# A retention layer and two MLPs on one core: six units of attention in plain float32, and no arithmetic on GpSimd

## The chip, the cores and the metric

The kernel runs on one core of one Trainium2 chip. A core has a matrix engine (TensorE, PE in the rows), a vector engine (VectorE, DVE), a scalar engine (ScalarE, ACT), GpSimd (POOL) and SyncE (SP), which here only issues transfers. Each engine takes its own instructions strictly in the order in which the program lists them, and waits on semaphores for the others. The metric is the device time of one execution in microseconds; lower is better. Before the change three runs gave 1268.5 to 1269.55 us, median 1269.53 us.

## The reference

```python
def _attn_ref(q, k, v):                     # B, H, S, D = 4, 8, 768, 64
    gamma = 1.0 - 2.0 ** (-5.0 - np.arange(H))
    for t in range(S):
        state = gamma * state + outer(k[t], v[t])       # one 64x64 state for each batch entry and head
        y[t] = (1 / sqrt(D)) * q[t] @ state
...
x = attn.transpose(0, 2, 1, 3).reshape(3072, 512)
h = x @ w_in;  x = np.maximum(0.01 * h, h) @ w_out      # first MLP, 512 -> 2048 -> 512
h = np.maximum(x @ w_in2, 0);  return (h * h) @ w_out2  # second MLP
```

The MLP weights arrive as float64, and the kernel makes float32 of them on the chip.

## The kernel before, in words

**Attention.** The recurrence is done in chunks of 256 tokens. A *unit* is one chunk of one batch entry; there are 12 (units 0 to 3 are the first chunks of the four entries, 4 to 7 the second, 8 to 11 the third), each with four pairs of heads. For each pair a row of 128x1024 floats (q, k, v, and k the other way round) is loaded, `prep_pair` multiplies the decays into q and v, and then for each head: `scores` (k against q, two key blocks of 128 against 256 queries), `soften` (causal mask, on DVE), `values` (masked scores against v, plus the older state against q), and, after a pair's second head, `outer` (adds the chunk to the state) and `combine` (writes y into the MLP's input).

**Two ways of multiplying.** The first three units (`WHOLE = 3`) give PE plain float32 operands. The profile shows two records on PE for each such product. All other products take each operand as a sum of two `float32r` parts, high and low, and multiply three pairs of parts (or stack the parts along the contraction or the output, in the attention). The parts are made by a copy on ACT and a subtraction on DVE or GpSimd: `kh`/`kl`, `q2`, `v2`, the masked scores `ph_pl`, the state `w2`, the weights `wih`/`wil` and `woh`/`wol`, the activations `gh`/`gl`.

**MLPs.** Tokens go in six blocks of 512; each MLP passes over six blocks, each in 16 *steps* j of 128 hidden columns (the first block has 21 steps: its first five run once on 256 tokens and again on the others). A step has 12 products into `h` (L402), an activation (L416 to L427) and 12 into `acc` (L462). In all 197 steps. Units 0 to 3 are used by the first two blocks; after the first eight heads one head goes with each step, until step 77: unit 4 with steps 14 to 21, unit 5 with 22 to 29, units 6 to 11 with 30 to 77 (`place`).

**Weights.** `convert` makes float32 of a half tile (128x512) of float64: two ACT operations (L314, L315), three DVE operations (L316, L317, L320) and an integer addition (L324), which is GpSimd's for the first MLP and for half of the second's half tiles, otherwise DVE's. The 32 half tiles of the first MLP are converted in the first steps, the second's from step 81 on, in block 5. `split_w` makes the two parts of a weight tile for every step anew; the subtraction (L365) is GpSimd's in the first block of each MLP, else DVE's. `soften`'s subtraction (L203) is GpSimd's in unit 3.

**Order.** The loops are written step by step; a scheduler then orders the instructions of each engine, so the rows of an engine are not in the order of the code. SP's queue takes the weight loads (`sg`) and the pairs' rows (`r`, `re`, `kn`) in one line.

Of the kernel before, what the change touches and what calls it, by code (L numbers as in the profile page):

```python
# [14 lines left out]
ALU = mybir.AluOpType  # L15
# [10 lines left out]
T = 512                      # tokens in a block of the MLPs  # L26
# [4 lines left out]
WHOLE = 3                    # units whose products are taken in float32 as it is: PE has the time for it then  # L31
HS = 5                       # steps of the first block on its first unit alone, in float32 as it is too
LEAD = 6                     # steps by which the heads run ahead of the block that takes them
AHEAD = 2                    # steps by which the first MLP's weights run ahead
AHEAD2 = 4                   # and the second's
PARTS = 4                    # units from which on GpSimd leaves the scores' parts to DVE
FLOOR = 2.0 ** -15 * 1.125   # its float32 pattern is the high word of float64's 2^-126

# columns of one pair's row in `attn`: q^T | k^T twice | v | k
Q0, K0, V0, N0, AW = 0, 256, 768, 1024, 1280  # L40
FW = 1024                    # the same, with k^T once, of a row in `first`
# [3 lines left out]
def retention_then_two_mlps(  # L45
# [27 lines left out]
    ph_pl = [const.tile([P, 2, 512], F32R, name=f"ph_pl{h}") for h in range(2)]  # L73
    state = const.tile([P, B, NP, D], F32, name="state")

# [18 lines left out]
    def load_pair(up):  # L94
        u, p = up
        k = ups.index(up)
        if u < WHOLE:
            if k % 4:
                t = slot(k % 4, [P, FW], F32, "re")
            else:  # L100
                t = a_p.tile([P, FW], F32, tag="r", name="r", bufs=1)
            if k == 0:
                nc.sync.dma_start(out=t[:, 0:2 * C], in_=first[k, :, 0:2 * C])
                nc.sync.dma_start(out=t[:, 2 * C:FW], in_=first[k, :, 2 * C:FW])
            else:
                nc.sync.dma_start(out=t, in_=first[k])
            raw[up] = (t[:, 0:C], t[:, C:2 * C], t[:, 2 * C:3 * C], t[:, 3 * C:FW])
            return
        row = attn[k - WHOLE * NP]
        t = a_p.tile([P, N0], F32, tag="r", name="r", bufs=1)  # L110
        nc.sync.dma_start(out=t, in_=row[:, 0:N0])
        kn = None
        if chunk(u) < NC - 1:
            kn = a_p.tile([P, 2 * P], F32, tag="kn", name="kn")
            nc.sync.dma_start(out=kn, in_=row[:, N0:AW])
        raw[up] = (t[:, Q0:K0], t[:, K0:V0], t[:, V0:N0], kn)

    def prep_pair(up):
        """Decays go to the queries and values; all but the first units' operands in two parts."""
# [11 lines left out]
        if u < WHOLE:  # L131
            prep[up] = (qs, k, vs)
            return
        kr = k.rearrange("p (h s) -> p h s", h=2)
        kh = [a_p.tile([P, C], F32R, tag="kh", name="kh") for h in range(2)]
        kl = [a_p.tile([P, C], F32R, tag="kl", name="kl") for h in range(2)]
        q2 = [a_p.tile([P, C], F32R, tag="q2", name="q2", bufs=3) for h in range(2)]
        v2 = [a_p.tile([P, 2, 2, D], F32R, tag="v2", name="v2", bufs=3) for h in range(2)]
        for h in range(2):
            nc.scalar.copy(kh[h], kr[:, h])  # L140
        for h in range(2):
            nc.vector.tensor_tensor(out=kl[h], in0=kr[:, h], in1=kh[h].bitcast(F32), op=ALU.subtract)  # L142
# [8 lines left out]
        for h in range(2):  # L151
            nc.scalar.copy(v2[h][:, :, 0], vs[:, :, h])
        for h in range(2):
            nc.vector.tensor_tensor(
                out=v2[h][:, :, 1], in0=vs[:, :, h], in1=v2[h][:, :, 0].bitcast(F32), op=ALU.subtract
            )
# [15 lines left out]
    def scores(hu):  # L172
        u, p, h = hu
        if u < WHOLE:
            qs, k, vs = prep[u, p]
            a = slice(64 * h, 64 * h + 64)
            sc = ps_h.tile([P, 512], F32, tag="h", name="sc")
            nc.tensor.matmul(out=sc[:, 128:256], lhsT=k[a, P:2 * P], rhs=qs[a, P:2 * P], start=True, stop=True)
            nc.tensor.matmul(out=sc[:, 256:512], lhsT=k[a, 0:P], rhs=qs[a], start=True, stop=True)
        else:  # L180
            q2, kh, kl, v2, vs, w2 = prep[u, p]
            sc = ps_h.tile([P, 512], F32, tag="h", name="sc")
            for sb in (1, 0):
                o = C * (1 - sb)
                for n, kk in enumerate((kh, kl)):
                    nc.tensor.matmul(  # L186
                        out=sc[:, o:o + C], lhsT=kk[h][:, sb * P:(sb + 1) * P], rhs=q2[h],
                        start=n == 0, stop=n == 1,
                    )
        sc_ps[hu] = sc  # L190

    def soften(hu):
        """Scores under the causal mask."""
        sc = sc_ps.pop(hu)
        pm = a_p.tile([P, 384], F32, tag="pm", name="pm")
        nc.vector.tensor_tensor(out=pm, in0=sc[:, 128:512], in1=mk, op=ALU.mult)  # L196
        if hu[0] < WHOLE:
            p_sb[hu] = pm
            return
        t = ph_pl[hu[2]]  # L200
        nc.scalar.copy(t[:, 0, 128:512], pm)
        eng = nc.gpsimd if hu[0] < PARTS else nc.vector
        eng.tensor_tensor(  # L203
            out=t[:, 1, 128:512], in0=pm, in1=t[:, 0, 128:512].bitcast(F32), op=ALU.subtract
        )

    def values(hu):
# [3 lines left out]
        if u < WHOLE:  # L211
# [3 lines left out]
            nc.tensor.matmul(out=y, lhsT=vs[:, 0, h], rhs=pm[:, 128:384], start=True, stop=False)  # L215
# [5 lines left out]
        if w2 is not None:  # L221
            nc.tensor.matmul(out=y, lhsT=w2[:, h].rearrange("p a e -> p (a e)"), rhs=q2[h], start=True, stop=False)
            start = False
        for n in range(2):
            for sb in range(2):
                o = C * (1 - sb)
                nc.tensor.matmul(  # L227
                    out=y, lhsT=v2[h][:, sb].rearrange("p a e -> p (a e)"), rhs=ph_pl[h][:, n, o:o + C],
# [4 lines left out]
    def outer(up):  # L233
        """Adds the chunk's keys and values to the state."""
# [61 lines left out]
    def convert():  # L296
        """The nearest float32 of a half tile of float64, out of its two words.

        The high word has the sign, the exponent and 20 bits of the fraction. Its
        pattern, as a float, keeps the order of the magnitudes and is held at or  # L300
        above that of 2^-126, the least that float32 holds. The low word, rounded
        to its upper three bits, is added to that as an integer.
        """
# [3 lines left out]
        if half == 0:  # L307
# [6 lines left out]
        nc.scalar.activation(out=r, in_=hi.bitcast(F32), func=AF.Abs)  # L314
        nc.scalar.activation(out=lo, in_=lo, func=AF.Copy, scale=2.0 ** -29)  # L315
        nc.vector.tensor_scalar(out=r, in0=r, scalar1=FLOOR, scalar2=None, op0=ALU.max)  # L316
        nc.vector.tensor_scalar(  # L317
            out=ru, in0=ru, scalar1=3, scalar2=0x3FFFFFF8, op0=ALU.logical_shift_left, op1=ALU.bitwise_and,
        )
        nc.vector.scalar_tensor_tensor(  # L320
            out=ru, in0=hi, scalar=0xC0000000, in1=ru, op0=ALU.bitwise_and, op1=ALU.bitwise_or,
        )
        eng = nc.vector if lay == 1 and (m % 4 < 2) else nc.gpsimd
        eng.tensor_tensor(out=ru, in0=ru, in1=lo, op=ALU.add)  # L324
# [10 lines left out]
    # a step: (layer block, j, first and last column)  # L335
# [10 lines left out]
    widens = {HS}                # the step where old and new columns meet  # L346
# [7 lines left out]
    def split_w(i, half):  # L354
# [9 lines left out]
        eng = nc.gpsimd if n in (0, NB) else nc.vector  # L364
        eng.tensor_tensor(out=lo, in0=src, in1=hi.bitcast(F32), op=ALU.subtract)  # L365
# [64 lines left out]
    def emit_out(i):  # L430
# [14 lines left out]
        # a bank's first product clears it for all its columns, also those of later steps  # L445
# [69 lines left out]
    conv2 = first_step[NB - 1]   # from here on the first MLP's weights go, tile by tile  # L515
# [5 lines left out]
    def after(hu):  # L521
        """What follows a head's values."""
# [16 lines left out]
    for t in ph_pl:  # L539
        nc.gpsimd.memset(t[:, :, 0:128].bitcast(F32), 0.0)  # L540
# [20 lines left out]
    for i in range(N):  # L561
# [27 lines left out]
        elif i >= conv2 - AHEAD2:  # L589
            j = i - conv2  # L590
            converted_to(2 * NJ + min(int((j + AHEAD2) / 0.85), 2 * max(j, 0) + 2))
# [5 lines left out]
def _tables():  # L597
    """Decays of the heads and the causal mask: of shapes alone."""
# [54 lines left out]
```

## Time and profile before

| | |
|---|---|
| median of three runs | 1269.53 us (1268.5 to 1269.55) |
| span of the profiled execution, first to last instruction | 1267.9 us; 0.6 to 1.7 us of a run's time lie around such a span |
| busy: PE, weight loads, DVE, ACT, POOL | 95%, 78%, 72%, 56%, 14% of the span |
| POOL instructions | 126, all before 220 us or between 620 and 860 us |
| PE matmul records | 5660 |

Matmuls are pipelined, so the mean duration of a record is longer than its pace; the distance between the starts of neighbours, or the time of a run of many, shows the pace. DVE instructions, too, are recorded some 0.08 us longer than the distance at which they follow each other. A block of the MLPs is 16 steps, so the distance between the last products of two blocks shows what a block took.

### The profile page before, as it was taken

Reading aid. Unit: us, or ns where it says so; the run is one execution under the profiler, and the core shown is the slowest. Engines: PE = TensorE matmul, PEld = TensorE weight load, DVE = VectorE, ACT = ScalarE, POOL = GpSimd, SP = SyncE. Lnnn points to the kernel's source line nnn. Section 1 sums busy time; section 2 is a strip of 40 time slices with the busy share of each in tenths; the row PEclk is TensorE's granted clock in tenths of the full one; section 3 lists DMA queues with packets and bytes.
Section 4 is the critical chain, followed back from the end, with each engine's and each line's share of the span. In section 5 each row is a group of like instructions: output and inputs, shape, how many; then the busy total and the mean of one; then the engine's idle time right before and its main releaser. Section 6 shows DMA issues by size and latency. Waiting matters only on the chain.

```text
span 1267.9 us, 15585 instructions
## 1 busy us (share of the span) xinstructions
PE 1210.7 (95%) x5660; PEld 995.2 (78%) x5660; DVE 915.9 (72%) x1669; ACT 711.3 (56%) x1482; POOL 171.7 (14%) x126
## 2 busy tenths in 40 slices
PE   6887797999999999999999989999999999999998
PEld 4566586888888888888887768888888888888886
DVE  5999988988988988898599972454555644555543
ACT  4555655766766776776467754444444544444443
POOL 1266662000000000000012264400000000000000
PEclk9898898999999999999999999999999999999999
DMA  8534211121111111111034410000000000000000
GB/s 296 200 136 161 98 59 42 42 63 42 42 59 34 34 50 34 41 44 50 1 99 151 150 50 1 1 34 1 1 34 1 34 1 1 34 1 1 34 1 33
DMA packets 23404, 69.36 MB, mean 55 GB/s; under 512 B 2848, under 2 KB 5664, under 8 KB 23328
## 3 DMA queue, kind: packets, MB, share of 16 engines
q1 hardware_dynamic: 23328, 68.37, 15.6%
q8 instruction: 44, 0.72, 0.2%
q14 instruction: 32, 0.26, 0.1%
HBM read 62.07 MB, written 6.29 MB: 54 GB/s over the span
## 4 chain that ended last, share of the span: by engine, by line
PE 78%; DVE 15%; issue 4%; DMA 2%; ACT 1%; SPq 0%; POOL 0%; DVEq 0%; ACTq 0%; POOLq 0%
PE acc L462 36%; PE h L402 35%; DVE w L320 3%; PE y L227 2%; PE sc L186 2%; DVE w L317 2%; DVE w L316 2%; DVE gl L427 1%; DVE pm L196 1%; DVE g L417 1%; DMA r<-attn 1%; DVE kl L142 1%; DVE q L148 1%; DVE qs L124 1%; DVE vs L125 1%
## 5 line engine op out<-in xcount | busy, mean ns | idle before, releaser
L402 PE MATMUL h<-xh,wih 128*128 128x512 f32 (+1 forms) x768 | 303.2, 395 | 11.8 <-DVE pm L196 9.3
L402 PE MATMUL h<-xh,wil 128*128 128x512 f32 (+1 forms) x768 | 302.7, 394 | 4.3 <-POOL wil L365 2.4
L402 PE MATMUL h<-xl,wih 128*128 128x512 f32 (+1 forms) x768 | 301.0, 392 | 0.1
L363 ACT CAST woh<-w 128x512 fp32r<-128x512 f32 x192 | 119.3, 622 | 161.2 <-PE acc L462 159.5
L365 DVE TENSOR_TENSOR wol<-w,woh 128x512 fp32r<-128x512 f32 x160 | 111.0, 694 | 118.4 <-ACT woh L363 117.2
L402 PEld LDWEIGHTS h<-xh,wih 128*128 128x128 f32 x768 | 147.0, 191 | 43.3 <-DVE pm L196 10.2
L402 PEld LDWEIGHTS h<-xh,wil 128*128 128x128 f32 x768 | 147.2, 192 | 36.8 <-DVE wil L365 4.7
L402 PEld LDWEIGHTS h<-xl,wih 128*128 128x128 f32 x768 | 146.7, 191 | 30.5 <-DVE xl L381 1.1
L427 DVE TENSOR_TENSOR gl<-g,gh 128x512 fp32r<-128x512 f32 (+1 forms) x192 | 144.9, 755 | 28.8 <-ACT gh L426 14.0
L426 ACT CAST gh<-g 128x512 fp32r<-128x512 f32 (+1 forms) x192 | 118.1, 615 | 59.6 <-DVE g L420 29.6
L324 POOL TENSOR_TENSOR w<-w,sg 128x512 uint32<-128x512 uint32 x48 | 70.2, 1464 | 575.3 <-DVE w L320 532.1
L420 DVE SCALAR_TENSOR_TENSOR g<-h,g 128x512 f32<-128x512 f32 x96 | 66.2, 690 | 89.0 <-ACT g L419 88.3
L363 ACT CAST wih<-w 128x512 fp32r<-128x512 f32 x192 | 117.8, 614 | 11.9 <-PE h L402 8.6
L365 DVE TENSOR_TENSOR wil<-w,wih 128x512 fp32r<-128x512 f32 x160 | 109.7, 686 | 5.8 <-ACT wih L363 5.5
L462 PE MATMUL acc<-gl,woh 128*128 128x512 f32 (+1 forms) x388 | 107.3, 386 | 4.2 <-DVE gl L427 4.2
L462 PE MATMUL acc<-gh,woh 128*128 128x512 f32 (+1 forms) x388 | 107.3, 390 | 1.6 <-ACT gh L426 1.5
L462 PE MATMUL acc<-woh,gh 128*128 128x512 f32 x384 | 105.7, 389 | 1.1 <-DVE ys L472 1.1
L419 ACT ACTIVATE g<-h 128x512 f32<-128x512 f32 x96 | 57.4, 598 | 87.7 <-PE h L402 80.2
L462 PE MATMUL acc<-gh,wol 128*128 128x512 f32 (+1 forms) x388 | 106.1, 383 | 0.0
L462 PE MATMUL acc<-wol,gh 128*128 128x512 f32 x384 | 105.6, 389 | 0.0
L462 PE MATMUL acc<-woh,gl 128*128 128x512 f32 x384 | 105.6, 389 | 0.0
L416 ACT ACTIVATE g<-h 128x512 f32<-128x512 f32 (+1 forms) x101 | 58.0, 575 | 70.2 <-PE h L402 42.6
(89 smaller groups left out, 1806.5 us busy)
## 6 DMA issues: line engine op xcount, KB each, us to landing
sg<-w SPq DMA_DIRECT2D x64, 512.0 KB, 3.6
r<-attn SPq DMA_DIRECT2D x36, 512.0 KB, 3.5
out<-os SPq DMA_DIRECT2D x24, 256.0 KB, 2.0
re<-first SPq DMA_DIRECT2D x9, 512.0 KB, 4.9
kn<-attn SPq DMA_DIRECT2D x20, 128.0 KB, 2.1
r<-first SPq DMA_DIRECT2D x2, 512.0 KB, 6.3
r<-first SPq DMA_DIRECT2D x2, 256.0 KB, 2.8
qt<-qtab SPq DMA_DIRECT2D x1, 384.0 KB, 6.4
```

What stands on the lines that cost most here:

```text
L186: nc.tensor.matmul(out=sc[:, o:o + C], lhsT=kk[h][:, sb * P:(sb + 1) * P], rhs=q2[h], start=n == 0, stop=n == 1,)
L320: nc.vector.scalar_tensor_tensor(out=ru, in0=hi, scalar=0xC0000000, in1=ru, op0=ALU.bitwise_and, op1=ALU.bitwise_or,)
L324: eng.tensor_tensor(out=ru, in0=ru, in1=lo, op=ALU.add)
L363: nc.scalar.copy(hi, src)
L365: eng.tensor_tensor(out=lo, in0=src, in1=hi.bitcast(F32), op=ALU.subtract)
L402: nc.tensor.matmul(out=hp[:, :c1 - c0], lhsT=a[:, kb * P:(kb + 1) * P], rhs=b[:, c0:c1], start=kb == 0 and k == 0, stop=kb == KB - 1 and k ...
L416: nc.scalar.activation(out=g[:, :m], in_=hp[:, :m], func=AF.Copy, scale=LEAK)
L419: nc.scalar.activation(out=g[:, :m], in_=hp[:, :m], func=AF.Relu)
L420: nc.vector.scalar_tensor_tensor(out=g[:, :m], in0=hp[:, :m], scalar=0.0, in1=g[:, :m], op0=ALU.max, op1=ALU.mult)
L426: nc.scalar.copy(gh[:, :m], g[:, :m])
L427: nc.vector.tensor_tensor(out=gl[:, :m], in0=g[:, :m], in1=gh[:, :m].bitcast(F32), op=ALU.subtract)
L462: nc.tensor.matmul(out=o, lhsT=lhsT, rhs=rhs, start=start and k == 0, stop=stop and k == 2)
```

## The change

- `WHOLE` is 6: units 3, 4 and 5 also take plain float32 products, without parts. Units 4 and 5 have an older state; it is copied by ACT onto the two diagonal blocks of a 128x128 tile (`s_diag`, two of them, cleared once by GpSimd), and one product of 256 columns for both heads of a pair adds its part to y.
- The rows of units 4 and 5 are loaded in turn into `r` and one of the free block slots (before: `r` alone).
- `convert` has three DVE operations: ACT now scales the high word by a power of two in place of taking its magnitude, the maximum (L316) is gone, the shift has no mask, and the integer addition is always DVE's.
- `split_w`'s and `soften`'s subtractions are always DVE's. GpSimd only clears the two tiles.
- In the units still split, the second key block is multiplied with the 128 queries that can see it (before: 256, of which 128 were masked to zero), in scores and values. `kh`/`kl` and `v2` are made for two heads in one operation each.
- The second MLP's half tiles are converted at one a step (before: 1.18 a step), with a due time.

```diff
-WHOLE = 3
+WHOLE = 6
-    ph_pl = [const.tile([P, 2, 512], F32R, name=f"ph_pl{h}") for h in range(2)]
+    s_diag = [const.tile([P, P], F32, name=f"s_diag{n}") for n in range(2)]
@@ load_pair
-            if k % 4:
-                t = slot(k % 4, [P, FW], F32, "re")
+            if k % 4 and (k < 4 * NP or k % 2):
+                t = slot(k % 4 if k < 2 * NP else 2 + k % 2 if k < 4 * NP else 3, [P, FW], F32, "re")
@@ prep_pair
         if u < WHOLE:
+            if chunk(u):
+                for h in range(2):
+                    a = slice(64 * h, 64 * h + 64)
+                    nc.scalar.copy(s_diag[p % 2][a, a], state[a, u % B, p])
@@ scores
             for sb in (1, 0):
-                o = C * (1 - sb)
+                o, c = (P, P) if sb else (C, 0)
                 for n, kk in enumerate((kh, kl)):
                     nc.tensor.matmul(
-                        out=sc[:, o:o + C], lhsT=kk[h][:, sb * P:(sb + 1) * P], rhs=q2[h],
+                        out=sc[:, o:o + C - c], lhsT=kk[:, h * C + sb * P:h * C + (sb + 1) * P], rhs=q2[h][:, c:C],
@@ values
+            if past and h == 0:
+                nc.tensor.matmul(out=y_ps[u, p][:, 0], lhsT=s_diag[p % 2], rhs=qs, start=True, stop=False)
...
-                    out=y, lhsT=v2[h][:, sb].rearrange("p a e -> p (a e)"), rhs=ph_pl[h][:, n, o:o + C],
+                    out=y[:, c:C], lhsT=v2[:, sb, h].rearrange("p a e -> p (a e)"), rhs=t[:, n, o:o + C - c],
@@ convert
-        nc.scalar.activation(out=r, in_=hi.bitcast(F32), func=AF.Abs)
+        nc.scalar.activation(out=r, in_=hi.bitcast(F32), func=AF.Copy, scale=2.0 ** -112)
-        nc.vector.tensor_scalar(out=r, in0=r, scalar1=FLOOR, scalar2=None, op0=ALU.max)
-        nc.vector.tensor_scalar(
-            out=ru, in0=ru, scalar1=3, scalar2=0x3FFFFFF8, op0=ALU.logical_shift_left, op1=ALU.bitwise_and,
-        )
+        nc.vector.tensor_scalar(out=ru, in0=ru, scalar1=3, scalar2=None, op0=ALU.logical_shift_left)
-        eng = nc.vector if lay == 1 and (m % 4 < 2) else nc.gpsimd
-        eng.tensor_tensor(out=ru, in0=ru, in1=lo, op=ALU.add)
+        nc.vector.tensor_tensor(out=ru, in0=ru, in1=lo, op=ALU.add)
@@ split_w
-        eng = nc.gpsimd if n in (0, NB) else nc.vector
-        eng.tensor_tensor(out=lo, in0=src, in1=hi.bitcast(F32), op=ALU.subtract)
+        nc.vector.tensor_tensor(out=lo, in0=src, in1=hi.bitcast(F32), op=ALU.subtract)
@@ the order of it all
-            converted_to(2 * NJ + min(int((j + AHEAD2) / 0.85), 2 * max(j, 0) + 2))
+            due = 2 * (i + 1 + AHEAD - first_step[NB]) + 1
+            converted_to(2 * NJ + max(min(j + AHEAD2, 2 * max(j, 0) + 2), due))
```

How this stands in the engines' orders, at two places. The first is DVE in the first steps, where half tiles of weights are converted (`w`) between the heads of the first units (`pm` is a head's masked scores, `qs`/`vs` a pair's decayed operands, `xl` a part of the MLP's input). Before:

```order
L316 TENSOR_SCALAR w<-w 128x512
L317 TENSOR_SCALAR w<-w 128x512
L316 TENSOR_SCALAR w<-w 128x512
L125 TENSOR_TENSOR vs<-re,vt 128x256
L317 TENSOR_SCALAR w<-w 128x512
L320 SCALAR_TENSOR_TENSOR w<-sg,w 128x512
L196 TENSOR_TENSOR pm<-sc,mk 128x384
L317 TENSOR_SCALAR w<-w 128x512
L196 TENSOR_TENSOR pm<-sc,mk 128x384
L124 TENSOR_TENSOR qs<-re,qt 128x256
L320 SCALAR_TENSOR_TENSOR w<-sg,w 128x512
```

And now, in the same steps:

```order
L314 TENSOR_SCALAR w<-w 128x512
L315 SCALAR_TENSOR_TENSOR w<-sg,w 128x512
L124 TENSOR_TENSOR vs<-re,vt 128x256
L192 TENSOR_TENSOR pm<-sc,mk 128x384
L374 TENSOR_TENSOR xl_551<-xs_137,xh_550 128x512
L315 SCALAR_TENSOR_TENSOR w<-sg,w 128x512
L318 ISA w<-sg,w 128x1024
L192 TENSOR_TENSOR pm<-sc,mk 128x384
L123 TENSOR_TENSOR qs<-re,qt 128x256
L318 ISA w<-sg,w 128x1024
L314 TENSOR_SCALAR w<-w 128x512
```

One of the two scalar operations of a half tile is gone from DVE, and GpSimd's integer addition stands there now (the `ISA` rows, 128x1024 half words).

The second place is PE in a step of units 6 and later, around one split head (`sc` scores, `y` values, `w` the older state, `sp` the outer product). Before:

```order
L186 MATMUL sc<-q_3681,kh 128x256
L186 MATMUL sc<-q_3681,kl 128x256
L243 MATMUL sp<-vs,kn 128x128 x2
L462 MATMUL acc<-gh,woh 128x512 x4
L462 MATMUL acc<-gh,wol 128x512 x2
L222 MATMUL y<-q_3680,w_3696 128x256
L227 MATMUL y<-ph_pl_89,v_3682 128x256 x4
L222 MATMUL y<-q_3681,w_3696 128x256
```

And now:

```order
L182 MATMUL sc<-q_2470,kh 128x128
L182 MATMUL sc<-q_2470,kl 128x128
L182 MATMUL sc<-q_2470,kh 128x256
L182 MATMUL sc<-q_2470,kl 128x256
L224 MATMUL y<-ph,v_2320 128x256
L224 MATMUL y<-ph,v_2320 128x128
L455 MATMUL acc<-gh,woh 128x512 x4
L455 MATMUL acc<-gh,wol 128x512 x4
L455 MATMUL acc<-gl,woh 128x512 x4
```

Of the eight products of a head's scores and values four now have 128 columns; there are 192 such products in the 48 heads of units 6 to 11.

## Rows read from the trace of the kernel before

**Rows 1.** Stages: length; busy (count) of PE, PEld, DVE, ACT, POOL; clock, DMA, GB/s

```profile
0.00:20.00 20.00, 12.14 (x54) 7.72 (x55) 6.06 (x16) 7.45 (x18) 0.77 (x6) 1.00 0.86 318
20.00:160.00 140.00, 114.78 (x522) 84.99 (x522) 135.78 (x201) 81.28 (x172) 74.30 (x54) 0.88 0.44 156
160.00:220.00 60.00, 52.23 (x303) 44.73 (x302) 50.91 (x99) 34.88 (x90) 25.05 (x19) 0.94 0.17 53
...
240.00:640.00 400.00, 400.00 (x2009) 339.82 (x2008) 337.49 (x748) 267.15 (x639) 0.15 (x1) 1.00 0.13 41
640.00:750.00 110.00, 101.60 (x424) 79.41 (x422) 107.55 (x174) 74.33 (x132) 35.95 (x22) 0.98 0.38 129
```

**Rows 2.** Chain that ended last, in order of time: start, length, what

```profile
161.29 3.57 DMA r<-attn
...
649.03 5.44 PE acc L462 x24
...
750.28 4.84 PE acc L462 x20
...
837.41 5.44 PE acc L462 x24
```

**Rows 3.** Timeline, 64.9 to 66.6 us: start, length, engine, line

```profile
64.94 1.35 POOL L324 TENSOR_TENSOR w<-w,sg 128x512 uint32<-128x512 uint32 x1 [2.15 <-DVE w L320]
65.06 1.51 DVE L317 TENSOR_SCALAR w<-w 128x512 uint32<-128x512 uint32 x1
```

**Rows 4.** Timeline, 71.3 to 72.5 us, DVE

```profile
71.36 0.68 DVE L320 SCALAR_TENSOR_TENSOR w<-sg,w 128x512 uint32<-128x512 uint32 x1
71.96 0.41 DVE L316 TENSOR_SCALAR w<-w 128x512 f32<-128x512 f32 x1
...
72.30 0.54 DVE L196 TENSOR_TENSOR pm<-sc,mk 128x384 f32<-128x384 f32 x1
```

**Rows 5.** Groups by line on DVE, 0 to 220 us: busy us, mean ns

```profile
L317 DVE TENSOR_SCALAR w<-w 128x512 uint32<-128x512 uint32 x33 | 31.6, 957 | 0.4
...
L427 DVE TENSOR_TENSOR gl<-g,gh 128x512 fp32r<-128x512 f32 x11 | 14.8, 1343 | 0.3 <-ACT gh L426 0.3
```

**Rows 6.** Groups by line on DVE, 240 to 640 us

```profile
L365 DVE TENSOR_TENSOR wol<-w,woh 128x512 fp32r<-128x512 f32 x62 | 42.8, 690 | 7.6 <-ACT woh L363 6.4
L427 DVE TENSOR_TENSOR gl<-g,gh 128x512 fp32r<-128x512 f32 x61 | 41.7, 684 | 0.9 <-ACT gh L426 0.2
...
L142 DVE TENSOR_TENSOR kl<-r,kh 128x256 fp32r<-128x256 f32 x53 | 22.0, 415 | 0.0
...
L317 DVE TENSOR_SCALAR w<-w 128x512 uint32<-128x512 uint32 x2 | 0.9, 427 | 0.1
L324 DVE CUSTOM_DVE_ANT_0 w<-sg,w 128x1024 uint16<-128x1024 uint16 x1 | 0.7, 681 | 0.0
```

**Rows 7.** Groups by line on POOL, 0 to 220 us

```profile
L324 POOL TENSOR_TENSOR w<-w,sg 128x512 uint32<-128x512 uint32 x32 | 44.9, 1404 | 80.6 <-DVE w L320 46.8 <-DMA sg<-w 20.0 <-ACT gh L426 4.0
```

**Rows 8.** Timeline on PE, two stretches: one plain head, one split head's scores

```profile
75.41 0.65 PE L215 MATMUL y<-pm,vs 128*64 128x256 f32 x2
75.89 0.38 PE L216 MATMUL y<-pm,vs 128*64 128x128 f32 x2
76.20 0.48 PE L178 MATMUL sc<-qs,re 64*128 64x128 f32 x2
76.53 0.59 PE L179 MATMUL sc<-qs,re 64*128 64x256 f32 x2
...
105.41 0.28 PE L186 MATMUL sc<-q,kh 128*128 128x256 f32 x1
105.53 0.28 PE L186 MATMUL sc<-q,kl 128*128 128x256 f32 x1
```

**Rows 9.** Groups by line on PE, 0 to 220 us

```profile
L402 PE MATMUL h<-xh,wih 128*128 128x512 f32 (+1 forms) x71 | 30.6, 431 | 9.3 <-DVE pm L196 9.3
```

**Rows 10.** The page's part 4, by engine

```profile
PE 78%; DVE 15%; issue 4%; DMA 2%; ACT 1%; SPq 0%; POOL 0%; DVEq 0%; ACTq 0%; POOLq 0%
```

More of the change, by code (lines that the diff above doesn't have):

```diff
@@ L35 @@
 AHEAD2 = 4
-PARTS = 4
-FLOOR = 2.0 ** -15 * 1.125
 Q0, K0, V0, N0, AW = 0, 256, 768, 1024, 1280
@@ L131, in prep_pair @@
         if u < WHOLE:
+            if chunk(u):
+                for h in range(2):
+                    a = slice(64 * h, 64 * h + 64)
+                    nc.scalar.copy(s_diag[p % 2][a, a], state[a, u % B, p])
             prep[up] = (qs, k, vs)
             return
-        kr = k.rearrange("p (h s) -> p h s", h=2)
-        kh = [a_p.tile([P, C], F32R, tag="kh", name="kh") for h in range(2)]
-        kl = [a_p.tile([P, C], F32R, tag="kl", name="kl") for h in range(2)]
+        kh = a_p.tile([P, 2 * C], F32R, tag="kh", name="kh", bufs=1)
+        kl = a_p.tile([P, 2 * C], F32R, tag="kl", name="kl", bufs=1)
         q2 = [a_p.tile([P, C], F32R, tag="q2", name="q2", bufs=3) for h in range(2)]
[L138 to L142, printed above, removed]
+        v2 = a_p.tile([P, 2, 2, 2, D], F32R, tag="v2", name="v2", bufs=2)
+        nc.scalar.copy(kh, k)
+        nc.vector.tensor_tensor(out=kl, in0=k, in1=kh.bitcast(F32), op=ALU.subtract)
         for h in range(2):
@@ L150, in prep_pair @@
             )
[L151 to L155, printed above, removed]
-            )
+        nc.scalar.copy(v2[:, :, :, 0], vs)
+        nc.vector.tensor_tensor(out=v2[:, :, :, 1], in0=vs, in1=v2[:, :, :, 0].bitcast(F32), op=ALU.subtract)
         w2 = None
@@ L199, in soften @@
             return
[L200 to L205, printed above, removed]
+        t = p_sb[hu] = a_p.tile([P, 2, 384], F32R, tag="ph", name="ph")
+        nc.scalar.copy(t[:, 0], pm)
+        nc.vector.tensor_tensor(out=t[:, 1], in0=pm, in1=t[:, 0].bitcast(F32), op=ALU.subtract)
     def values(hu):
@@ L214, in values @@
             y = y_ps[u, p][64 * h:64 * h + 64, 0]
-            nc.tensor.matmul(out=y, lhsT=vs[:, 0, h], rhs=pm[:, 128:384], start=True, stop=False)
+            past = chunk(u) > 0
+            if past and h == 0:
+                nc.tensor.matmul(out=y_ps[u, p][:, 0], lhsT=s_diag[p % 2], rhs=qs, start=True, stop=False)
+            nc.tensor.matmul(out=y, lhsT=vs[:, 0, h], rhs=pm[:, 128:384], start=not past, stop=False)
             nc.tensor.matmul(out=y[:, P:2 * P], lhsT=vs[:, 1, h], rhs=pm[:, 0:128], start=False, stop=True)
@@ L223, in values @@
             start = False
+        t = p_sb.pop(hu)
         for n in range(2):
             for sb in range(2):
-                o = C * (1 - sb)
+                c, o = (P, 0) if sb else (0, P)
                 nc.tensor.matmul(
-                    out=y, lhsT=v2[h][:, sb].rearrange("p a e -> p (a e)"), rhs=ph_pl[h][:, n, o:o + C],
+                    out=y[:, c:C], lhsT=v2[:, sb, h].rearrange("p a e -> p (a e)"), rhs=t[:, n, o:o + C - c],
                     start=start, stop=n == 1 and sb == 1,
@@ L313, in convert @@
         ru = r.bitcast(U32)
-        nc.scalar.activation(out=r, in_=hi.bitcast(F32), func=AF.Abs)
+        nc.scalar.activation(out=r, in_=hi.bitcast(F32), func=AF.Copy, scale=2.0 ** -112)
         nc.scalar.activation(out=lo, in_=lo, func=AF.Copy, scale=2.0 ** -29)
-        nc.vector.tensor_scalar(out=r, in0=r, scalar1=FLOOR, scalar2=None, op0=ALU.max)
-        nc.vector.tensor_scalar(
-            out=ru, in0=ru, scalar1=3, scalar2=0x3FFFFFF8, op0=ALU.logical_shift_left, op1=ALU.bitwise_and,
-        )
-        nc.vector.scalar_tensor_tensor(
-            out=ru, in0=hi, scalar=0xC0000000, in1=ru, op0=ALU.bitwise_and, op1=ALU.bitwise_or,
-        )
-        eng = nc.vector if lay == 1 and (m % 4 < 2) else nc.gpsimd
-        eng.tensor_tensor(out=ru, in0=ru, in1=lo, op=ALU.add)
+        nc.vector.tensor_scalar(out=ru, in0=ru, scalar1=3, scalar2=None, op0=ALU.logical_shift_left)
+        nc.vector.scalar_tensor_tensor(
+            out=ru, in0=hi, scalar=0x80000000, in1=ru, op0=ALU.bitwise_and, op1=ALU.bitwise_or,
+        )
+        nc.vector.tensor_tensor(out=ru, in0=ru, in1=lo, op=ALU.add)
         if n_loaded[0] < 2 * NJ or lay == 1:
@@ L538, in retention_then_two_mlps @@
     load_half()
-    for t in ph_pl:
-        nc.gpsimd.memset(t[:, :, 0:128].bitcast(F32), 0.0)
+    for t in s_diag:
+        nc.gpsimd.memset(t, 0.0)
     first_acc = ps_acc.tile([P, 4, T], F32, tag="acc", name="first_acc")
```

## The prediction

> **What bounds the kernel now.** I read the stages first, then the chain, then groups of instructions. From 240 to 640 us PE is busy all 400 us, and the chain of the whole run is 78% PE [rows 1, 10]: there a PE microsecond added or removed is a microsecond of the time. Two stages are different. From 20 to 160 us DVE is busy 135.8 of 140 us, PE only 114.8, and at a mean clock of 0.88 (its two levels are 1.2 and 2.4 GHz); POOL works 74 us there. From 640 to 750 us DVE is busy 107.6 of 110 us, PE 101.6, POOL 36 [rows 1]. In both, the reader sees DVE full just where POOL works. Why it is full, the timeline shows: a scalar operation on DVE that starts while POOL adds takes 1.51 us and ends 0.28 us after POOL [rows 3]; where POOL rests the same operation averages 427 ns [rows 6]. In the groups of 0 to 220 us it averages 957 ns over 33, `gl` 1343 ns against 684 over 11 [rows 5, 6]. That is 33 x 0.530 = 17.5 us and 11 x 0.659 = 7.2 us of standing still; done for the eleven groups that have a slow mean it comes to 60 us. Across the 72 POOL operations there (32 additions [rows 7], 32 subtractions of weights, 8 of scores) that is 0.8 us each.
>
> What this costs: a step's products take 24 x 5.44/24 = 5.44 us [rows 2] (the piece at 837.41). Counting all products in PE's order up to the `h` of step 22 at 0.227 us (512 columns), 0.118 (256 columns, from the distance of two neighbours [rows 8]) and the plain ones at four times that (0.48 for 256 [rows 8]), PE had 147 us of work to do; the 71 of 72 first-kind `h` records that lie before 220 us [rows 9] say that it took about 218 us. So 71 us are lost there: 12 at the start, before there is anything to multiply, the rest to DVE and to a clock at half speed. In block 5 the distance between the last products of two blocks is 750.3 - 649.0 = 101.3 us, in block 6 it is 87.1 [rows 2]: 14 us lost.
>
> **The change part by part.**
>
> *First stage, DVE.* Busy 192.8 us before 220 us [rows 1]. POOL's operations go, and with them the 60 us of stalls: 133 left. Removed: 33 maxima at 0.42 [rows 4], 14 us; the parts of units 3 and of the first pairs of 4 (16 parts of k at 0.415 [rows 6], as many of q and 12 joins of y alike, 16 of v with half the columns at 0.28, six of scores with 384 columns like the mask's 0.54 [rows 4]), 26 us. Added: 32 integer additions at 0.681 and 32 subtractions at 0.69 [rows 6], 44 us. That leaves 137 us; with the 14 us that DVE idles at the start, it could be through at 151 us.
>
> *First stage, PE.* Units 3 and most of 4 in plain float32: a head costs 0.33 + 0.53 for scores and 0.48 + 0.31 for values [rows 8], about half of the values' time beside the other head where both come together, so 1.25 to 1.65 us; a split head with scores and values of eight products at 0.118 costs 0.94, and 1.06 with the older state. 15 heads change kind here: +5 to +12 us, work of 152 to 159 us, and 12 us of start. PE could be there at 164 to 171 us. Now neither engine is far ahead, DVE at 151, PE at 168. They hand work to each other for each head and each step, so I add 14 us for that (from 60 us of loss beyond the start before, of which DVE's stalls no longer count): step 22 at 184 us in place of 218, **-34 us**. Bounds: 166 (nothing lost, -52) and 203 (half the loss stays, -15).
>
> *Steps 22 to 29.* PE is the bound. Nine heads in plain float32 at 1.25 to 1.65 us, and a quarter of a microsecond each for the product with the diagonal tile (half of 0.48), in place of 1.06: 0.83 more in the middle, +7.5; the last 2 us of DVE's lateness before 240 us go: **+5.5 us** (+2 to +8).
>
> *Units 6 to 11.* 192 products have 128 columns in place of 256. The trace has no `float32r` product under 256. From below: 512 and 256 columns take 227 and 118 ns, on a line through both 128 take 64, -54 ns each, -10 us. If the weights' load sets the pace, nothing is gained: 118. From above: like plain float32, half of 0.48, 240 ns, +122 each, +23 us. I take 91, between the two ends that are of the same kind of product, as the nearer rows: **-5 us**. On the weights' load a rule speaks against this edit. The Trainium skill, "TensorE: Matmul & The Clock Gate", section "LDWEIGHTS (loading the stationary operand)", gives a load 1/1.2 ns a column whatever the contraction, 107 ns for 128, and its section "Weight-path perf modes" keeps the faster load from float32 weights. By that rule a narrow product would take some 107 ns, an estimate from that page, and the edit would bring 2 us; the 118 ns of 256 columns agrees with both, so no row here decides.
> The merged `kl` and `v2` take some 12 us off DVE over 24 pairs; PE is the bound, so nothing.
>
> *Block 5.* 28 half tiles stand between the first activations of blocks 5 and 6 in DVE's order, each 0.34 + 0.60 + 0.60 at the pace of neighbours [rows 4]; with 73 other operations at 0.60 that is 43 + 44 = 87 us, against PE's 87. No stalls. So DVE is just full, and I keep 5 of the 14 us: **-9 us** (-14 to 0). Block 6 has 32 subtractions more on DVE, 19 us, where it was busy under half of the time; nothing.
>
> *Elsewhere.* ACT has less to do. GpSimd's loss costs nothing. SP's queue: the rows of units 3 to 5 are loaded into two buffers in turn in place of one; they still stand in line behind weight loads that wait for a conversion. Before, the chain had three waits for such a row, of 3.6 us (the first in [rows 2]); I count no gain.
>
> Sum: -34 + 5.5 - 5 - 9 = -42.5. The span was 1267.9 us, some 1.6 under the median of the runs. 1225.4 + 1.6 gives **1227 us**; its own range, 1212 to 1240.
>
> **Rivals.**
>
> *Narrow products are slow.* Every 128-column `float32r` product costs as a plain one: 23 us in place of -5, in the stage where PE is the bound. 1227 + 28 = 1255. For it: plain products show four times the pace for the same columns [rows 8], and no row shows a narrow one of the other kind. Against it: their pace falls in proportion from 512 to 256 columns.
>
> *The first stage only half follows.* DVE no longer bounds it, but the round for a head (scores, mask, values, y, state, one buffer for y) does, and the clock falls again in the gaps. 17 us of the 34: 1244. For it: with 114.8 of 140 us busy PE ran at 0.88 [rows 1]. Against it: DVE has 16 us of slack now.
>
> *Late rows of q, k and v: slower.* A plain unit holds its row until the outer product, since k and the scores read it directly, and the next row waits behind that on SP, in line with the weights. If each of the 16 pairs of units 2 to 5 waits for one landing, 3.6 us [rows 2], that is 57 us: 1284. It decides from 42.5/16 = 2.7 us a pair. For it: the three waits that are there already. Against it: two buffers in turn, and a step of 5.4 us for each head, so a pair lasts three landings.
>
> *More than I count.* First stage at its bound, block 5 without loss, narrow products at 64 ns: -52 + 2 - 10 - 14 = -74, 1195; half way there, 1211.
>
> **How the numbers follow.** Forecast 0.48; narrow products slow 0.18; half the stage 0.20; more 0.08; late rows 0.06. What is within 0.2%, 2.5 us either way, can't be told from no change; only two bad cases together come there (slow products and a stage that hardly moves: 1227 + 28 + 17 = 1272). Faster 0.91, same 0.03, slower 0.06. The range reaches down into "more", up past the slow products: 1202 to 1260, leaving out the late rows, half of "more" and the part of slow products that comes with half the stage.
>
> **What would show it.** Right: no DVE operation of 512 columns over 0.8 us in the first stage, the shift at 0.42; step 22's `h` near 184 us; block 5 within 5 us of block 6; pairs of steps with split heads from unit 6 on shorter by 0.2 us. Wrong: a 128-column product at a distance of 118 ns or more to its neighbour; waits of PE or DVE for `r` or `re` of several us in steps 5 to 30; DVE still full to 160 us without POOL, which would mean that POOL did not make its operations long.

## The result, and the profile after

The changed kernel took 1237.63 us (median of four runs, 1236.55 to 1239.77), the kernel before 1269.54 beside it: ratio 0.9749, 95% interval 0.9735 to 0.9763. Faster by 31.9 us; 42.5 were forecast, and 1237.6 lies inside the forecast's own range. The profiled execution's span is 1236.4 us, 31.5 less than before.

The stages of the changed kernel, in the columns of [rows 1]:

```profile
20.00:160.00 140.00, 133.71 (x631) 95.58 (x630) 110.09 (x215) 82.80 (x166) 0.00 (x0) 0.96 0.46 161
160.00:220.00 60.00, 60.00 (x322) 46.21 (x321) 36.04 (x78) 24.39 (x53) 0.00 (x0) 1.00 0.14 45
...
240.00:640.00 400.00, 399.96 (x1981) 334.73 (x1980) 326.66 (x666) 257.24 (x561) 0.00 (x0) 1.00 0.14 43
640.00:750.00 110.00, 109.37 (x478) 89.07 (x477) 91.84 (x160) 73.29 (x130) 0.00 (x0) 1.00 0.33 106
```

DVE is no longer full in any of them. PE is, to within two per cent, from 60 us on, and its clock from 20 to 160 us is 0.96 where it was 0.88. The clock is below full speed only between 40 and 60 us, at a mean of its two levels:

```profile
40.00:60.00 20.00, 16.36 (x74) 10.43 (x73) 18.71 (x40) 12.58 (x28) 0.00 (x0) 0.74 0.66 236
```

There PE was busy 15.86 us at the same clock of 0.74 before the change, so up to 60 us PE has won about nothing. DVE's groups of 0 to 190 us say why it is no longer full:

```profile
L314 DVE TENSOR_SCALAR w<-w 128x512 uint32<-128x512 uint32 x33 | 13.7, 422 | 1.9 <-ACT w L312 1.8
...
L420 DVE TENSOR_TENSOR gl<-g,gh 128x512 fp32r<-128x512 f32 x11 | 7.6, 688 | 0.9 <-ACT gh L419 0.7
```

The shift takes 422 ns in place of 957 and `gl` 688 in place of 1343 [rows 5].

To see where the 31.5 us come from, I follow one instruction, DVE's second copy out of `acc` (`ys`), which stands at the end of each block of the first MLP. Its rows in the timelines of before, at the ends of blocks 0, 1, 4 and 5:

```profile
228.62 0.69 DVE L472 COPY ys<-acc 128x512 f32<-128x512 f32 x1
...
339.35 0.69 DVE L472 COPY ys<-acc 128x512 f32<-128x512 f32 x1
...
646.10 0.68 DVE L472 COPY ys<-acc 128x512 f32<-128x512 f32 x1
...
749.55 0.68 DVE L472 COPY ys<-acc 128x512 f32<-128x512 f32 x1
```

and of the changed kernel:

```profile
198.38 0.68 DVE L465 COPY ys<-acc 128x512 f32<-128x512 f32 x1
...
319.57 0.69 DVE L465 COPY ys<-acc 128x512 f32<-128x512 f32 x1
...
626.91 0.69 DVE L465 COPY ys<-acc 128x512 f32<-128x512 f32 x1
...
718.36 0.68 DVE L465 COPY ys<-acc 128x512 f32<-128x512 f32 x1
```

| stretch | before, us | after, us | difference | forecast |
|---|---|---|---|---|
| to the end of block 0 (units 0 to 3, most of 4) | 228.6 | 198.4 | -30.2 | -34 (to step 22) |
| block 1 (last head of unit 4, unit 5, most of 6) | 110.7 | 121.2 | +10.5 | +5.5 |
| blocks 2 to 4 (the rest of units 6 to 11) | 306.8 | 307.3 | +0.6 | -5 (with unit 6) |
| block 5 (the second MLP's weights) | 103.5 | 91.5 | -12.0 | -9 |
| from there to the end of the span | 518.4 | 518.0 | -0.3 | 0 |

The forecast's own mark for the first stage is another: the 72nd `h` record of the first kind, which belongs to step 22. It starts at 220.0 us before ([rows 9] have 71 of them up to 220 us) and at 194.6 us after. By this mark the first stage is 25.4 us shorter, and from there to the end of block 1 the change costs 5.7 us. The sum of the two is the same as in the table, because block 0 ended 8.6 us after that record before and ends 3.8 us after it now.

### The profile page after: what moved, and what is told of

It is laid out like the page before. It is cut to its first block, busy times and chain, and to the rows that moved or that the text cites. A ratio compares the mean times of both kernels' runs of the same rounds, so it can differ in the third digit from the quotient of the medians.

```text
span 1236.4 us, 15059 instructions
## 1 busy us (share of the span) xinstructions
PE 1215.3 (98%) x5660; PEld 984.2 (80%) x5660; DVE 834.0 (67%) x1541; ACT 668.5 (54%) x1310; POOL 0.6 (0%) x6
## 4 chain that ended last, share of the span: by engine, by line
PE 90%; DMA 4%; DVE 3%; ACT 2%; issue 1%; SPq 0%; ACTq 0%; DVEq 0%
PE acc L455 39%; PE h L395 39%; DMA sg<-w 3%; PE y L211 2%; PE sc L182 2%; PE y L224 1%; PE sc L175 1%; PE sp L240 1%; PE sc L174 1%; DVE w L318 1%; PE h L385 1%; DVE w L315 1%; PE y L212 1%; ACT w L312 1%; PE acc L432 1%
## 5 line engine op out<-in xcount | busy, mean ns | idle before, releaser
L395 PE MATMUL h<-xh,wil 128*128 128x512 f32 (+1 forms) x768 | 298.6, 389 | 0.0
L395 PE MATMUL h<-xl,wih 128*128 128x512 f32 (+1 forms) x768 | 297.8, 388 | 0.4 <-DVE xl L374 0.4
L358 DVE TENSOR_TENSOR wol<-w,woh 128x512 fp32r<-128x512 f32 x192 | 132.4, 690 | 155.6 <-ACT woh L357 154.4
L395 PEld LDWEIGHTS h<-xh,wih 128*128 128x128 f32 x768 | 144.3, 188 | 31.7 <-issue 2.8
L395 PEld LDWEIGHTS h<-xh,wil 128*128 128x128 f32 x768 | 144.3, 188 | 29.4 <-DVE wil L358 1.7
L420 DVE TENSOR_TENSOR gl<-g,gh 128x512 fp32r<-128x512 f32 (+1 forms) x192 | 130.9, 682 | 28.7 <-PE acc L455 14.3
L358 DVE TENSOR_TENSOR wil<-w,wih 128x512 fp32r<-128x512 f32 x192 | 131.4, 685 | 10.2 <-ACT wih L357 9.8
L192 DVE TENSOR_TENSOR pm<-sc,mk 128x384 f32<-128x384 f32 x96 | 53.1, 555 | 46.0 <-PE sc L175 31.6
```

The costliest lines, as they stand in the source:

```text
L358: nc.vector.tensor_tensor(out=lo, in0=src, in1=hi.bitcast(F32), op=ALU.subtract)
L395: nc.tensor.matmul(out=hp[:, :c1 - c0], lhsT=a[:, kb * P:(kb + 1) * P], rhs=b[:, c0:c1], start=kb == 0 and k == 0, stop=kb == KB - 1 and k ...
L420: nc.vector.tensor_tensor(out=gl[:, :m], in0=g[:, :m], in1=gh[:, :m].bitcast(F32), op=ALU.subtract)
```

## The experiments

All times are medians of four runs; "before" beside them was 1269.3 to 1269.8 us. The theory (A): DVE stood still while GpSimd worked, and that was what cost time before; plain float32 units cost PE more than they are worth once PE is the bound.

**One part alone: no arithmetic on GpSimd.**

```diff
 # the kernel before
-        eng = nc.vector if lay == 1 and (m % 4 < 2) else nc.gpsimd
+        eng = nc.vector
...
-        eng = nc.gpsimd if n in (0, NB) else nc.vector
+        eng = nc.vector
...
-        eng = nc.gpsimd if hu[0] < PARTS else nc.vector
+        eng = nc.vector
```

> The kernel before with one part of the change alone: GpSimd's additions and subtractions are DVE's, all else as before (three units plain, four scalar or logical operations and an addition for each half tile, wide products). Theory A (DVE stood still while GpSimd worked, and that was the first stage's and block 5's loss): the slow means fall to those of 240 to 640 us, DVE has 167 us of work up to step 22 and passes it at some 185 to 190 us in place of 218, block 5 is 8 to 11 us shorter, the whole 1226 to 1240 us. Rival B (the first stage became shorter because three units lost their parts): DVE takes on 112 operations more and keeps its load, the whole 1255 to 1275 us.

Measured 1239.44 us, ratio 0.9772 (0.975 to 0.9795): 30 of the 32 us with this part alone, as theory A had it. By the `ys` copies in this run's timeline, 24.5 us of them are won by the end of block 0 and 6.3 us in block 5, where 8 to 11 were expected. Its stages:

```profile
20.00:160.00 140.00, 122.79 (x602) 91.36 (x600) 131.99 (x286) 93.27 (x199) 0.00 (x0) 0.96 0.47 164
160.00:220.00 60.00, 54.62 (x335) 48.65 (x334) 55.94 (x138) 43.14 (x107) 0.00 (x0) 0.97 0.17 51
...
640.00:750.00 110.00, 105.36 (x452) 85.25 (x451) 96.69 (x179) 70.28 (x124) 0.00 (x0) 0.98 0.33 106
```

From 20 to 160 us DVE gets through 286 operations in 132 us; with GpSimd's help it did 201 in 136 [rows 1]. DVE is still the fuller engine there. Rival B is out as an account of the gain.

**GpSimd's presence, or its results?** Four units plain, and 128 additions on GpSimd on a tile that nobody else touches.

```diff
 # the changed kernel with WHOLE = 4
+    spare = const.tile([P, 2 * P], F32, name="spare")
...
         nc.vector.tensor_tensor(out=ru, in0=ru, in1=lo, op=ALU.add)
+        if lay == 0:
+            for _ in range(4):
+                nc.gpsimd.tensor_tensor(out=spare, in0=spare, in1=spare, op=ALU.add)
```

> The kernel with four units plain (1227 us), and GpSimd given 128 additions of 128x256 on a tile of its own that nobody else reads, writes or waits for; they start with the kernel and run one after the other. Theory A (DVE's operations with two operands in SBUF, or in its fast mode, stand still while GpSimd works, whoever's the data): for as long as the additions run DVE's shift and its 256-column products take up to one GpSimd operation longer, the mask (one operand in PSUM) does not, and the first stage loses 15 us or more: 1240 us or more. Rival C (what cost time before was waiting for GpSimd's results, at 1.4 us an operation, and not its presence): DVE's means stay at 0.42 and 0.42 us and the time at 1225 to 1229 us.

Measured 1252.45 us against 1226.95 for the same kernel without them: 25.5 us lost, though nothing waits for GpSimd. Nearly all of it is lost in the first stage: the `ys` copy at the end of block 0 starts at 223.1 us with the additions and at 198.4 us without. DVE's groups of 0 to 110 us with the additions:

```profile
L316 DVE SCALAR_TENSOR_TENSOR w<-sg,w 128x512 uint32<-128x512 uint32 x22 | 22.2, 1014 | 0.0
L319 DVE CUSTOM_DVE_ANT_0 w<-sg,w 128x1024 uint16<-128x1024 uint16 x21 | 21.3, 1030 | 0.1
L315 DVE TENSOR_SCALAR w<-w 128x512 uint32<-128x512 uint32 x23 | 18.5, 813 | 0.0
L193 DVE TENSOR_TENSOR pm<-sc,mk 128x384 f32<-128x384 f32 x22 | 11.9, 545 | 2.4 <-PE sc L176 2.4
```

and without:

```profile
L315 DVE SCALAR_TENSOR_TENSOR w<-sg,w 128x512 uint32<-128x512 uint32 x30 | 20.3, 685 | 0.0
L318 DVE CUSTOM_DVE_ANT_0 w<-sg,w 128x1024 uint16<-128x1024 uint16 x29 | 19.5, 686 | 0.1
L192 DVE TENSOR_TENSOR pm<-sc,mk 128x384 f32<-128x384 f32 x27 | 14.8, 552 | 3.9 <-PE sc L175 3.9
L314 DVE TENSOR_SCALAR w<-w 128x512 uint32<-128x512 uint32 x31 | 13.0, 423 | 2.6 <-ACT w L312 2.5
```

The shift (`TENSOR_SCALAR`) and the operations with two operands in SBUF take 0.33 to 0.39 us longer; the mask, with one operand in PSUM, does not. Rival C is out: GpSimd works 100.5 us here, as long as in the kernel before (100.1 us up to 220 us [rows 1]), and 24.7 us are lost by the end of block 0, about as much as the run without GpSimd won there (24.5). The Trainium skill says the same in "SBUF — State Buffer", section "Who interferes with whom": DVE's operations with two inputs in SBUF, and its two-port modes, which the shift's operation (`tensor_scalar`) can enter, contend with GpSimd for a shared pair of ports, and an operation with one input in SBUF outside those modes does not; in a two-port mode whoever issues first holds the pair for the whole instruction. The runs agree on which operations become longer and which does not; of a single wait [rows 3] shows one, a shift that ended 0.28 us after GpSimd's addition.

**Two parts: and the conversion in three operations and no mask.** The kernel with no arithmetic on GpSimd, and the changed `convert`:

```diff
-        nc.scalar.activation(out=r, in_=hi.bitcast(F32), func=AF.Abs)
+        nc.scalar.activation(out=r, in_=hi.bitcast(F32), func=AF.Copy, scale=2.0 ** -112)
...
-        nc.vector.tensor_scalar(out=r, in0=r, scalar1=FLOOR, scalar2=None, op0=ALU.max)
...
```

> The kernel before with two parts of the change: no arithmetic on GpSimd, and the conversion in three DVE operations and an addition less the maximum and the mask. 64 maxima of 0.34 us go from DVE, 33 of them in the first stage, where without GpSimd it is still busy 132 of 140 us. If DVE bounds that stage (theory A), 7 to 11 us less there and 3 to 5 us in block 5: 1224 to 1230 us. If it no longer does, 1237 to 1240 us as with GpSimd's part alone.

Measured 1227.91 us (0.9668, 0.9654 to 0.9683): another 11.5 us, as expected where DVE is the bound. The shares are not as expected: by the `ys` copies 4.4 us are won by the end of block 0, where the clock from 20 to 60 us also rose from 0.87 to 0.96, and 6.6 in block 5; 7 to 11 and 3 to 5 had been expected. These two parts alone are 10 us faster than the whole change.

**The same part taken out of the changed kernel.**

```diff
 # the changed kernel
...
+        nc.vector.tensor_scalar(out=r, in0=r, scalar1=FLOOR, scalar2=None, op0=ALU.max)
...
```

> The changed kernel with the conversion's maximum and mask back on DVE (the addition stays there), six plain units. Theory A: PE is full from 60 us on and DVE half idle after 120 us, so of 64 x 0.34 = 22 us DVE work little is seen: up to 4 us before 60 us and 2 to 5 us in block 5, where DVE is busy 92 of 110 us: 1239 to 1246 us. If DVE still bounds both stages: 1250 to 1258 us.

Measured 1240.94 us: 3.3 us lost, little more than the scatter of these runs (1238.9 to 1243.5), where the same part was worth 11.5 with three units plain. With six, PE is the bound in the first stage and DVE's microseconds count for nothing there: block 0 ends at 195.5 us, no later than in the changed kernel (198.4). In block 5 they still count: it takes 96.7 us in place of 91.5.

**Fewer plain units.** `WHOLE = 4`, then 3, in the changed kernel.

```diff
-WHOLE = 6
+WHOLE = 4
```

> The changed kernel with WHOLE = 4 in place of 6: units 4 and 5 go back to parts, the diagonal tiles are not used. Theory A (PE is full from 60 us on, and a plain head costs it about 2.3 us in place of 1.1): 16 heads give back 1.2 us each, 1237 - 19, so 1216 to 1222 us, block 1 near 111 us in place of 121. Rival B (DVE needs those units plain, 40 us of parts come back to it): DVE full again before step 22, 1237 to 1255 us.

Measured 1226.95 us (0.9665, 0.9645 to 0.9685): 10.7 us better than six. Of the 19 expected half came: block 0 ends at 198.4 us as with six, and PE now waits again (PE and DVE are each busy 54 of 60 us before 220 us), but block 1 takes 109.3 us in place of 121.2. Rival B's range, 1237 and more, is missed by 10 us; theory A's by 5.

> The changed kernel with WHOLE = 3: units 3, 4 and 5 have parts again. Theory A: unit 3's eight heads free 8 us of PE before step 22, and give DVE 14 us, which in the run with four plain units was busy 54 of 60 us before 220 us; so against 1227 us for four plain units nothing or a little lost, 1224 to 1232 us. If DVE's slack counts (rival B) 1240 us or more; if PE alone counts, 1218 us.

Measured 1227.0 us, as with four. That unit 3 in parts gives PE about what it costs DVE is the likely reason; no run shows it. Against the two parts alone (1227.9 us, also with three units plain) the rest of the change (narrow products, merged parts, buffers, the order of the second MLP's weights) comes to 0.9 us, within the noise.

**The pace of a narrow product.** The scores' 256-column products of the first key block, each made as two of 128 columns:

```diff
-            for sb in (1, 0):
-                o, c = (P, P) if sb else (C, 0)
+            for sb, o, c in ((1, P, P), (0, C, 0), (0, C + P, P)):
                 for n, kk in enumerate((kh, kl)):
```

> The changed kernel in which the scores' 256-column product of the first key block is made as two of 128 columns with the same weights: 96 products of 256 columns become 192 of 128, columns and results the same. If the load of the weights sets the pace (each product at least some 117 ns to the next), 96 more products cost 11 us: 1247 to 1250 us. If a narrow product takes 64 ns: 96 x 10 ns, 1 us, 1238 us. At the 91 ns of the forecast: 6 us, 1243 us. If narrow ones run like plain float32 (240 ns): 96 x 362 ns, 35 us, 1272 us.

Measured 1247.55 us, 9.9 more: 103 ns for each of the 96 further products. Six narrow ones in a row, PE's timeline of that run:

```profile
466.20 0.22 PE L181 MATMUL sc<-q,kh 128*128 128x128 f32 x1
466.25 0.28 PE L181 MATMUL sc<-q,kl 128*128 128x128 f32 x1
466.37 0.27 PE L181 MATMUL sc<-q,kh 128*128 128x128 f32 x1
466.48 0.27 PE L181 MATMUL sc<-q,kl 128*128 128x128 f32 x1
466.59 0.27 PE L181 MATMUL sc<-q,kh 128*128 128x128 f32 x1
466.70 0.28 PE L181 MATMUL sc<-q,kl 128*128 128x128 f32 x1
466.82 1.15 PE L454 MATMUL acc<-gh,woh 128*128 128x512 f32 x4
```

After the first, 0.11 to 0.12 us from one to the next: hardly less than the distance of 256 columns (0.118). The loads of their weights start 0.11 us apart in the same trace. That the load sets the pace, and not some other cost of each product, is inferred from this and not shown. The same in the changed kernel, where narrow and wide stand in turn:

```profile
461.22 0.22 PE L182 MATMUL sc<-q,kh 128*128 128x128 f32 x1
461.28 0.28 PE L182 MATMUL sc<-q,kl 128*128 128x128 f32 x1
461.39 0.33 PE L182 MATMUL sc<-q,kh 128*128 128x256 f32 x1
461.56 0.28 PE L182 MATMUL sc<-q,kl 128*128 128x256 f32 x1
461.68 0.40 PE L395 MATMUL h<-xh,wih 128*128 128x512 f32 x1
```

The first narrow one is short (0.06), and the wide one behind the narrow pair takes 0.17 in place of 0.12: what is saved is given back at the next products. The four take 0.46 us; four wide ones take 0.47.

**And taken back in the scores.**

```diff
-                o, c = (P, P) if sb else (C, 0)
+                o, c = C * (1 - sb), 0
```

> The changed kernel with the scores' narrow products taken back (second key block against all 256 queries, 96 products), the values' narrow ones kept. If the weights' load sets the pace: no difference, 1236 to 1239 us. At the forecast's 91 ns: 96 x 27 ns, 2.6 us slower. At 64 ns: 5 us slower. Like plain float32: 12 us faster.

Measured 1238.29 us, 0.7 more than with narrow ones, not to be told from none.

**Plain heads side by side.** `WHOLE = 5`; both heads' scores in one step, both heads' values in the next.

```diff
+        if hu[0] < WHOLE:
+            k -= k % 2
         head_at.setdefault(max(0, place(k)), []).append(hu)
...
+            if len(both) == 2 and i > 0:
+                held.append(both)
+                continue
             for hu in both:
                 values(hu)
```

> The changed kernel with WHOLE = 5, and with the two heads of a plain pair in the same step: scores of both in one step, values of both one after the other in the next, so that their products lie side by side (units 0 and 1 did that before: four records of 256 columns in 0.48 us). Unit 5 back in parts gives 8 x 1.2 = 9.6 us; the values of 12 pairs at 0.8 us for two heads in place of 1.6, and half of the changes between kinds of products (0.1 us each), 11 to 14 us: 1214 to 1219 us. If the values don't overlap, or a plain head costs PE only what the forecast counted: 1226 to 1231 us.

Measured 1216.51 us, ratio 0.9578 (0.9564 to 0.9593): the fastest version, 21 us under the change. Its PE timeline:

```profile
151.41 0.66 PE L211 MATMUL y<-pm,vs 128*64 128x256 f32 x4
151.89 0.40 PE L212 MATMUL y<-pm,vs 128*64 128x128 f32 x4
152.22 0.71 PE L240 MATMUL sp<-vs,r 128*128 128x128 f32 x4
...
157.04 0.50 PE L174 MATMUL sc<-qs,re 64*128 64x128 f32 x4
157.37 0.61 PE L175 MATMUL sc<-qs,re 64*128 64x256 f32 x4
157.91 0.74 PE L455 MATMUL acc<-gh,woh 128*128 128x256 f32 x4
```

The values of two heads (four records in each row) take 0.81 us and the scores of two heads 0.87, about what those of one head take alone (0.79 and 0.84). That the range was hit is in part luck: the expectation counts the values of 12 pairs and no scores; from 60 us on the values of 6 pairs of 11 run side by side, and the scores of 8 of 10.

> The same with WHOLE = 6, as in the changed kernel: unit 5 plain, side by side. PE is the bound there, and a plain head side by side costs some 0.5 to 0.6 us more than one in parts: 1216.5 + 4 to 5, 1219 to 1223 us; so against the changed kernel (1237.6 us) placing the heads alone gives 15 to 18 us.

1218.95 us: 2.4 more than with five units, and 18.7 less than the changed kernel, by the placing of the heads alone.

> The run with plain heads side by side, with WHOLE = 4 in place of 5: unit 4 in parts. PE gains some 8 x 0.6 us before step 22, DVE gets 20 us more there, where with four units plain it was busy 54 of 60 us before 220 us. If DVE decides: 1216 to 1221 us; if PE does: 1210 to 1213 us.

1220.48 us, inside the range for the case that DVE decides: block 0 ends at 193.7 us where it ended at 184.8 with five units plain, and DVE is busy 54.7 of the 60 us before 220 us.

## Why the prediction was right in direction and 11 us too large

**First stage, DVE: right.** The stalls went as the rows of before had said: 60 us of them, and the means of the first stage are now those of the quiet stretch. The run with a spare tile shows that GpSimd's presence makes them, the run without GpSimd that taking them away was worth 30 us, 24.5 of them in this stage. That DVE would then have slack was right too: 24 us of the 60 between 160 and 220 us.

**First stage, PE: the price of a plain head was mis-sized.** This is the step that failed, here above all, and in "Steps 22 to 29". I had a plain head at 1.25 to 1.65 us, with about half of the values' time beside the other head, and 0.24 for the diagonal tile; 0.83 more than a split one, which I called the middle, though it is the upper end of these numbers (1.65 + 0.24 - 1.06; the middle is 0.63). PE's timeline in the changed kernel, where unit 5 is worked on:

```profile
220.05 0.39 PE L395 MATMUL h<-xl,wih 128*128 128x512 f32 x1
220.37 0.49 PE L174 MATMUL sc<-qs,re 64*128 64x128 f32 x2
220.69 0.59 PE L175 MATMUL sc<-qs,re 64*128 64x256 f32 x2
221.21 1.20 PE L455 MATMUL acc<-gh,woh 128*128 128x512 f32 x4
...
222.94 0.59 PE L210 MATMUL y<-qs,s_diag 128*128 128x256 f32 x2
223.18 0.59 PE L455 MATMUL acc<-gh,wol 128*128 128x512 f32 x1
223.61 1.09 PE L455 MATMUL acc<-gl,woh 128*128 128x512 f32 x4
...
226.14 0.39 PE L395 MATMUL h<-xh,wil 128*128 128x512 f32 x1
226.46 0.65 PE L211 MATMUL y<-pm,vs 128*64 128x256 f32 x2
226.94 0.38 PE L212 MATMUL y<-pm,vs 128*64 128x128 f32 x2
227.25 0.50 PE L395 MATMUL h<-xl,wih 128*128 128x512 f32 x1
227.59 0.40 PE L395 MATMUL h<-xh,wih 128*128 128x512 f32 x1
```

The values stand alone (0.48 + 0.31), because the two heads of a pair are in different steps, so nothing runs beside them. And where scores or values meet other products, some 0.1 us is lost: the `h` product before the scores takes 0.32 to the next and the one after the values 0.34, where 0.227 is the pace. The change from one kind of product to the other does not explain this. The product with the diagonal tile is plain too, but has weights of 128 rows and 128 columns (`128*128`; scores have `64*128`, values `128*64`), and nothing is lost around it: it and the `acc` product behind it take 0.67 us, and their paces, 0.48 and 0.227, make 0.71. With the scores' 0.84, half a diagonal product and four such losses a plain head costs about 2.3 us, some 1.2 more than a split one. In block 1 the change cost 10.5 us for nine heads, 1.17 each; against the run with four units plain, which differs in that block by these heads alone, it is 11.9 us, 1.32 each.

In the first stage PE was the bound from 60 us on, and the 72nd `h` record of the first kind starts at 194.6 us, not 184; all 72 lie before 195 us:

```profile
L395 PE MATMUL h<-xh,wih 128*128 128x512 f32 (+1 forms) x72 | 27.0, 375 | 0.0
```

At 1.2 us the 15 heads that change kind there cost 18 us, where I had 5 to 12. The sum has a slip as well: 168 and 14 make 182, not 184. The 14 us that I had added for the handing to and fro were lost in part, but not where heads and steps hand work to each other all through the stage: after 60 us PE did not wait at all. From 20 to 60 us it stood idle 6.3 us and its clock fell, as before the change; together that is some 10 us (an estimate: 16.4 us of work at 0.74 lose 4.3). So by the forecast's own mark the stage came out at -25 for -34. By the end of block 0 it is -30, which looks nearer only because that mark lies elsewhere in PE's order.

**Narrow products: the size.** I took 91 ns between 64 and 118; they pace at 103 to 114, and in the blocks of units 6 to 11 nothing was gained (+0.6 us for -5). The rule of the Trainium skill that I set beside it ("TensorE: Matmul & The Clock Gate", "LDWEIGHTS (loading the stationary operand)", an estimate of 107 ns) lies within what the runs show. The rival of a fourfold price is out.

**Block 5: right,** -12 for -9. DVE had 92 of 110 us to do, and PE lost less than 1 us in the same stretch; the block takes 91.5 us. GpSimd's rest alone brought 6.3 of it and the shorter conversion 6.6 more.

**The rivals.** "The first stage only half follows" gave 1244 us, which is nearer to the measured 1237.6 than the forecast's 1227, and by the forecast's own mark the stage gained 25 us, half way between this rival's 17 and the forecast's 34. What it describes, PE waiting and its clock falling in the gaps, is seen up to 60 us and not after: from there PE is busy all the time at a clock of 1.00. Late rows of q, k and v did not come about: after the first two loads no wait of DVE for `r` or `re` is left among the long ones in the first 240 us. What DVE waits for there is PE:

```profile
DVE pm L192 <- PE sc L175: 23.5, 15, 3.3
DVE vs L124 <- PE y L212: 16.8, 13, 4.3
```

(us in total, times, longest). That is the picture of the kernel before turned round. So, in the order in which the runs add the parts, GpSimd's rest is worth 30 us, the shorter conversion 11.5 on top, and the further plain units, which both of these made needless, take 10.7 back: units 4 and 5 all of it, unit 3 nothing.

## What to carry to other kernels

When an engine looks full, compare the mean of one operation between a stretch where its neighbour works and one where it rests; a difference there is not work, and taking the neighbour away can be faster than sharing with it. When one edit moves the bound to another engine, the edits made to spare the first engine must be priced again on the second: here two more plain units cost 10.7 us once DVE was no longer the bound, and placing the two heads of a pair side by side took 18.7 off. And before products are made narrower, measure whether the next one starts any sooner: here half the columns gained nothing.

## What the runs showed of the hardware

- A `float32r` product of 128 columns with its own weights paces at 103 to 114 ns, one of 256 at 118; with 192 products halved nothing was gained (+0.6 us over the three blocks that hold most of them), and a short one in front of a long one gives its gain back in the next distance.
- Plain products of two heads that use different halves of the array run side by side when they are neighbours in PE's order: 0.81 us for both heads' values (outputs in different halves of the partitions) and 0.79 for one head's; 0.87 for both heads' scores (inputs in different halves) and 0.84 for one head's. Heads in different steps paid the whole time each.
- Going from products that fill the array to plain ones that fill half of it (64 rows or 64 columns of weights), and back, cost about 0.1 us each way (0.32 to 0.34 us in place of 0.227). Going between `float32r` and plain float32 products that both fill it cost nothing (0.67 us for two products whose paces make 0.71).
- GpSimd additions of 128x256 (785 ns each) on a private tile made DVE's operations with two operands in SBUF 0.33 to 0.34 us longer on average and its one-operand shift 0.39 us, and one with an operand in PSUM no longer (545 ns for 552).
